# One PSUM tile for the scores of a head pair, with the first bias steps moved between engines and pools

## The chip, the cores and the metric

The kernel runs on one core of a Trainium2 chip. The metric is the device time of one execution in microseconds (us), lower is better. Engines are named as in the profile: PE (TensorE matmul), PEld (its weight loads), DVE (VectorE), ACT (ScalarE), POOL (GpSimd), SP (SyncE, which issues most transfers).

## What is computed

Attention with a learned bias from relative position, then a feed-forward layer. Sizes: 4 batches, 8 heads, 576 positions, head width 64; the feed-forward layer takes 2304 rows of 512 to 2048 and back.

```python
scores = scale * np.matmul(q, k.transpose(0, 1, 3, 2))
x = (np.log1p(np.abs(i - j)) / np.log1p(np.maximum(i, 1)))[..., None]
bias = np.maximum(x @ w1 + b1, 0.0) @ w2          # hidden width 32, 8 heads
scores = scores + bias.transpose(2, 0, 1)[None]
attn = softmax(scores); y = np.matmul(attn, v)    # softmax with its maximum taken off
h = y_rows @ w_in
out = (h / (1 + np.exp(-1.702 * h))) @ w_out
```

## The kernel before, in words

**Precision.** Products of 16-bit operands are made from a high and a low half (q, k, v, weights, softmax rows are each split into two fp16 parts), with three matmuls per product: high by high, high by low, low by high.

**Units.** The attention is cut into 72 units. A unit is one batch, one chunk of 128 query rows (the fifth chunk has 64) and one pair of heads; batches go in two groups of two, 36 units each. Chunks 0 to 3 have eight units in a group, the short chunk four, and a unit of the short chunk takes two pairs of heads. For unit u the loop at line 650 writes, in this order: a hidden step of the bias (`bias_first`), the scores (`emit_s`), the softmax (`emit_soft1`), in units 0 to 3 an extra half step of the bias, one feed-forward step, the product with v for unit u-3 (`emit_av`), another feed-forward step, the second half of the bias step (`bias_second`), the load of the bias rows for unit u+2, weight splits (`weights_to`), and what the dictionary `todo` holds for that unit (loads, transposes and splits of q, k and v).

**Who sets the order.** The written order is a priority. At build time a scheduler (`schedule_with_timeline_sim=True`, line 722) puts the instructions of each engine into a fixed order by its own cost model; on the chip every engine and every DMA queue runs its list in that order and waits where an operand or a buffer isn't ready.

**Scores.** `emit_s` takes two tiles of the PSUM pool `ps_s`, one for each head of the pair. Head 0 has its q and k in partitions 0 to 63, head 1 in partitions 64 to 127, so the matmuls of the two heads use different halves of the PE array's rows. Each head has six matmuls: three parts, each with 512 and with 64 columns (short chunk: twelve). They are written alternately, head 0, head 1, head 0, and so on. DVE then adds the bias rows and takes the extreme (L351), ACT makes the exponential (L358) and the high part (L365, some on DVE at L363), POOL the low part (L366), and a transposing DMA brings the result to `aT` (L371) for `emit_av`.

**PSUM.** `ps_s` has two buffers of two banks, with the tag "s". They are shared by the two score tiles, the transposes of q (`trans_q`) and k (`trans_k`, one head pair at a time) and the products of a bias step (`o`, L176). `ps_h` and `ps_o` have two buffers of one bank; `ps_o` holds the feed-forward output of a block from unit 11 on.

**Bias.** For each of the 36 bias steps (8 for each of four chunks, 4 for the short one) `bias_hidden` makes four hidden tiles, on ACT (L165) or DVE (L167) as the step's string in `BIAS_ENG` says (V or A), `bias_products` multiplies them by w2 on PE (L188 and L190), ACT moves the result out of PSUM (L195) and a DMA of ACT's queue writes it to a table `scr` in DRAM (L196). `bias_load` reads the rows for a unit back (L210, SP's queue). Steps 1 and 2 alone put their products into two one-bank tiles `om` and `ol` (`BIAS_PSUM`). Steps 0 to 7, needed by unit 0, run ahead of the loop, with the entries of `FIRST` written between them; steps 8 to 15 are written in units 0 to 3, two to a unit; the rest from unit 5 on, one to a unit, up to unit 28.

**Weights.** `split_w` loads (L439) and splits (L458, L461, L464, L470, L224) the feed-forward weights in 32 pieces, `W_STEPS` of them in each of units 0 to 11.

Of the kernel before, what the change touches and what calls it, by code (L numbers as in the profile page):

```python
# [7 lines left out]
F32 = mybir.dt.float32  # L8
# [12 lines left out]
def kernel(  # L21
# [26 lines left out]
    nc = tc.nc  # L48
# [21 lines left out]
    BIAS_ENG = ["VVVA" if x % 2 else "VVAA" for x in range(8)] + ["AAAA"] * 16 + ["VVAA"] * 12  # L70
    BIAS_PSUM = {1: "h", 2: "o"}
# [19 lines left out]
    ps_s = ctx.enter_context(tc.tile_pool(name="ps_s", bufs=2, space=PSUM))  # L91
# [80 lines left out]
    def bias_products(c, s, eng, hts, ostag):  # L172
        na = eng.count("A")
        where = BIAS_PSUM.get(8 * c + s)
        if where is None:
            o = ps_s.tile([128, 2, 512], F32, tag="s", name="o").rearrange("p a n -> p (a n)")  # L176
# [23 lines left out]
    def bias_load(u):  # L200
# [6 lines left out]
        for e in range(1 if c < 4 else 2):  # L207
            hh = 2 * (hp + e)
            po = slice(64 * e, 64 * e + scr[c].shape[0])
            nc.sync.dma_start(out=t[po, :], in_=scr[c][:, hh:hh + 2, :].rearrange("p h n -> p (h n)"))  # L210
# [30 lines left out]
    def trans_q(b, c):  # L241
        t = q_st.pop((b, c))
        n = t.shape[0]
        ps = ps_s.tile([128, 2, 512], F32, tag="s", name="qp")[:, 0, 0:NP * n]
# [24 lines left out]
    def trans_k(b, hp):  # L269
        t = k_st[b, hp // 2]  # L270
        ps = ps_s.tile([128, 2, 512], F32, tag="s", name="kp").rearrange("p a n -> p (a n)")
        for c in range(4):
            nc.tensor.transpose(ps[:, 128 * c:128 * c + 128], t[:, hp % 2, c, :], idn)
        nc.tensor.transpose(ps[:, SM:S], kt_st[b][:, hp, :], idn[:ST, :ST])
        d = stage([128, 2, S], F16, "kT", "kT")
        nc.scalar.activation(out=d[:, 0], in_=ps[:, 0:S], func=ACTF.Copy, scale=KS)
        lo_part(False, d[:, 1], ps[:, 0:S], KS, d[:, 0])
        kT[b, hp] = d
# [44 lines left out]
    def emit_s(u):  # L323
# [3 lines left out]
        ps = [  # L327
            ps_s.tile([128, 2, 512], F32, tag="s", name="sp").rearrange("p a n -> p (a n)") for a in range(2)
        ]
# [224 lines left out]
    def drain_to(j):  # L554
# [5 lines left out]
    FIRST = {1: (trans_k, 0, 0), 2: (trans_q, 0, 0), 4: (trans_k, 0, 1), 6: (split_v, 0, 0)}  # L560
    FIRST_UNITS = (
        (0, (trans_q, 1, 0)), (0, (trans_k, 1, 0)), (1, (trans_k, 1, 1)), (1, (load_k, 1, 1)), (2, (split_v, 1, 0)), (2, (trans_k, 0, 2)),
        (2, (load_v, 0, 1)), (3, (trans_k, 0, 3)), (4, (trans_k, 1, 2)), (4, (split_v, 0, 1)), (4, (load_v, 1, 1)),
        (5, (trans_k, 1, 3)), (6, (split_v, 1, 1)),
# [52 lines left out]
    for s in range(8):  # L617
        bias_step(0, s, BIAS_ENG[s], (HT0[(2 * s) % 4], HT0[(2 * s + 1) % 4]), ("os", "bt")[s // 2 % 2])
        if s in FIRST:
            FIRST[s][0](*FIRST[s][1:])  # L620
# [106 lines left out]
```

## Time and profile before

| | |
|---|---|
| median of the runs | 772.23 us (3 runs, 770.73 to 776.1) |
| profiled execution, its own time | 770.94 us |
| its span, first to last instruction | 769.1 us |
| PE busy | 676.4 us, 88% of the span |
| DVE, ACT, POOL busy | 452.3, 425.8, 336.0 us |
| mean granted TensorE clock | 0.923 of full |

The profile is of one execution. Busy time of an engine counts the time in which any of its instructions ran; pipelined matmuls overlap, so the mean duration of one is longer than its share of the busy time. A row of the timeline has the start, the length, the engine, the line, what is written and read, how many instructions were merged, and in brackets the idle time before it and what ended it. Times in a timeline count from the start of the span.

### The profile page before, as it was taken

The numbers are of one execution on the slowest core, as the hardware profiler recorded it, in microseconds if no ns is written. First come the engines' busy times: TensorE is split into PE (matmuls) and PEld (weight loads), VectorE is DVE, ScalarE is ACT, GpSimd is POOL, SyncE is SP. The second block draws the span as 40 slices with busy tenths as digits, with TensorE's granted clock in tenths as the row PEclk, the third lists the DMA queues.
The fourth block names the chain that finished last, engine by engine and source line by source line (L and its number), as shares of the span: only waits on it lengthen the run. The fifth ranks groups of instructions, "written<-read, shape, count | busy, mean of one in ns | idle before, by whom it ended". The sixth has DMA issues, their size and how long they took to land.

```text
span 769.1 us, 17254 instructions
## 1 busy us (share of the span) xinstructions
PE 676.4 (88%) x6648; PEld 413.7 (54%) x6648; DVE 452.3 (59%) x1228; ACT 425.8 (55%) x958; POOL 336.0 (44%) x431
## 2 busy tenths in 40 slices
PE   5347677667999999999999999789999998999997
PEld 2113333224565566566666665456666665667665
DVE  4756678998565565555578964335666564663221
ACT  6667785797566665654456545453544353443123
POOL 1311153423454465455445654436546454563222
PEclk9855675576999999999999999999999999999999
DMA  9766878999956866677588666666685676564000
GB/s 227 225 194 160 242 193 221 287 233 259 229 131 127 177 135 126 153 157 133 106 202 197 129 121 126 138 134 98 143 163 113 111 178 121 98 112 99 15 29 15
DMA packets 249843, 116.50 MB, mean 151 GB/s; under 512 B 229792, under 2 KB 234016, under 8 KB 249760
## 3 DMA queue, kind: packets, MB, share of 16 engines
q1 hardware_dynamic: 241808, 99.96, 62.1%
q10 hardware_dynamic: 7952, 15.43, 6.0%
q8 instruction: 52, 0.85, 0.5%
q14 instruction: 31, 0.25, 0.1%
HBM read 52.85 MB, written 15.34 MB: 89 GB/s over the span
## 4 chain that ended last, share of the span: by engine, by line
PE 58%; DMA 14%; DVE 8%; ACT 4%; issue 3%; POOL 1%; SPq 0%; ACTq 0%; POOLq 0%; DVEq 0%
PE hp L494 20%; PE op L523 20%; DMA aT<-hl 12%; PE sp L335 8%; PE ot L402 6%; DVE a L351 2%; PE ot L395 2%; PE o L188 2%; ACT a L358 1%; ACT hl L365 1%; DVE w L461 1%; DVE th L502 1%; DMA w<-in_moe_w_in_dram 1%; DVE w L464 1%; POOL hl L366 1%
## 5 line engine op out<-in xcount | busy, mean ns | idle before, releaser
L366 POOL TENSOR_TENSOR hl<-a,hl 128x576 f16<-128x576 f32 x142 | 184.4, 1306 | 227.8 <-ACT hl L365 142.9
L494 PE MATMUL hp<-xT,wi 128*128 128x256 f16 (+1 forms) x1920 | 216.1, 263 | 9.1 <-DVE th L502 5.4
L523 PE MATMUL op<-wo,gT 128*128 128x512 f16 x864 | 214.7, 380 | 8.9 <-ACT gT L507 7.1
L494 PEld LDWEIGHTS <-wi 128*128 128x128 f16 x1920 | 167.1, 98 | 50.7 <-issue 20.9
L510 POOL TENSOR_TENSOR gT<-th,gT 128x256 f16<-128x256 f32 (+1 forms) x160 | 101.8, 637 | 131.7 <-DVE gT L509 46.4
L358 ACT ACTIVATE a<-a,mx 128x576 f32<-128x576 f32 x144 | 110.5, 769 | 55.9 <-DVE mx L355 55.0
L351 DVE CUSTOM_DVE_ANT_0 a<-sp,bt 128x576 f32<-128x576 f32 x144 | 106.1, 752 | 41.2 <-PE sp L335 33.4
L502 DVE SCALAR_TENSOR_TENSOR th<-th,hp 128x256 f32<-128x256 f32 (+1 forms) x160 | 62.6, 392 | 114.6 <-ACT th L500 114.2
L335 PE MATMUL sp<-kT,qT 64*128 64x512 f16 (+2 forms) x960 | 114.9, 297 | 15.1 <-DVE kT L224 4.8
L523 PEld LDWEIGHTS <-gT 128*128 128x128 f16 x864 | 80.6, 98 | 80.6 <-ACT gT L507 8.4
L500 ACT ACTIVATE th<-hp 128x256 f32<-128x256 f32 (+1 forms) x160 | 57.0, 357 | 106.9 <-PE hp L494 96.1
L188 PE MATMUL o<-ht,pk 128*32 128x512 f32 x272 | 63.6, 787 | 33.2 <-DVE mx L351 16.9
L335 PEld LDWEIGHTS <-qT 64*128 64x128 f16 (+1 forms) x960 | 45.7, 100 | 78.5 <-issue 50.1
L365 ACT CAST hl<-a 128x576 f16<-128x576 f32 x103 | 67.3, 667 | 35.4 <-DMA aT<-hl 34.7
L165 ACT ACTIVATE ht<-tab,pk 128x576 f32<-128x576 f32 x100 | 81.4, 861 | 3.1 <-PE o L190 2.9
L402 PE MATMUL ot<-v,aT 128*128 128x64 f16 (+1 forms) x1920 | 77.2, 199 | 0.0
L402 PEld LDWEIGHTS <-aT 128*128 128x128 f16 (+1 forms) x1920 | 70.2, 104 | 5.3 <-issue 5.0
L509 DVE CAST gT<-th 128x256 f16<-128x256 f32 x112 | 53.0, 473 | 4.4 <-PE op L523 0.5
L417 POOL TENSOR_TENSOR xn<-xf,xn 128x128 f16<-128x128 f32 x72 | 34.2, 475 | 42.0 <-ACT xn L416 23.4
L416 ACT CAST xn<-xf 128x128 f16<-128x128 f32 x70 | 20.5, 293 | 47.5 <-DVE xf L409 46.3
L386 DVE TENSOR_SCALAR sm<-sm 128x2 f32<-128x2 f32 x72 | 23.9, 332 | 37.8 <-ACT a L358 37.6
L363 DVE CAST hl<-a 128x576 f16<-128x576 f32 x41 | 23.8, 585 | 30.3 <-DMA aT<-hl 21.3
(59 smaller groups left out, 537.4 us busy)
## 6 DMA issues: line engine op xcount, KB each, us to landing
bt<-scr SPq DMA_DIRECT2D x32, 576.0 KB, 4.4
scr<-os ACTq DMA_DIRECT2D x36, 288.0 KB, 3.1
w<-in_moe_w_in_dram SPq DMA_DIRECT2D x16, 512.0 KB, 4.8
w<-in_moe_w_out_dram SPq DMA_DIRECT2D x16, 512.0 KB, 5.2
k<-in_k_dram SPq DMA_DIRECT2D x32, 128.0 KB, 4.3
q<-in_q_dram SPq DMA_DIRECT2D x16, 256.0 KB, 4.4
out_dram<-ob ACTq DMA_DIRECT2D x16, 256.0 KB, 2.5
bt<-scr SPq DMA_DIRECT2D x8, 288.0 KB, 4.2
```

The costliest lines, as they stand in the source:

```text
L165: nc.scalar.activation(out=h, in_=tv, func=ACTF.Relu, bias=b1c, scale=sc[:, col:col + 1])
L188: nc.tensor.matmul(om[po], lhsT=w2b, rhs=h[:, :, 0:128], start=True, stop=True)
L335: nc.tensor.matmul(ps[a][64 * e:64 * e + m, cs], lhsT=qt[r, x, hp + e, 0:m], rhs=kT[b, hp + e][r, y, cs], start=i == 0, stop=i == 2,)
L351: nc.vector.tensor_tensor_reduce(out=at[:, cs], in0=s_ps.pop((u, a))[:, 0:S], in1=bt[:, cs], scale=-1.0 / BS, scalar=3.0e38, op0=ALU.add, ...
L358: nc.scalar.activation(out=at[:, cs], in_=at[:, cs], func=ACTF.Exp, scale=-1.0, bias=mx[:, a:a + 1], accum_out=sm[:, a:a + 1],)
L365: nc.scalar.copy(hl[:, 0, cs], at[:, cs])
L366: (nc.vector if a and u in VEC_EXP_LO else nc.gpsimd).tensor_tensor(out=hl[:, 1, cs], in0=at[:, cs], in1=hl[:, 0, cs], op=ALU.subtract)
L402: nc.tensor.matmul(o[po, 64 * a:64 * a + 64], lhsT=t[:, 9 * y + 5 * a + kb, po], rhs=vt[:, x, 384 * a + 64 * kb:384 * a + 64 * kb + 64], s ...
L494: nc.tensor.matmul(p[:, :n], lhsT=wi16[:, x, cc, 128 * f:128 * f + 128], rhs=r, start=i == 0, stop=i == 11,)
L502: nc.vector.scalar_tensor_tensor(out=g[:, :n], in0=th[:, :n], scalar=1.0, in1=p[:, :n], op0=ALU.add, op1=ALU.mult)
L510: nc.gpsimd.tensor_tensor(out=gt[:, 1, :n], in0=g[:, :n], in1=gt[:, 0, :n], op=ALU.subtract)
L523: nc.tensor.matmul(op_t[j, i], lhsT=gt[:, x, ts], rhs=wo16[:, f, y, :], start=f == 0 and n3 == 0, stop=f == NF - 1 and n3 == 2,)
```

## The change

The two score tiles of a unit become one tile of four banks, and `ps_s` has one such buffer in place of two of two banks. `trans_k` makes both head pairs of a loaded tile into the same kind of tile, so it is called half as often. Bias steps 1 to 19 all use the two one-bank tiles of `ps_o`; step 0 and steps 20 to 35 use the first two banks of a four-bank tile. All eight first steps have three hidden tiles on DVE and one on ACT (before, every second one had two and two). `trans_q(1, 0)`, `trans_k(1, 0)` and `split_v(0, 0)` are written behind the eight first steps and ahead of the loop. The bias rows of unit 0 are loaded by GpSimd's queue. In the loop the weight splits and `bias_first` are written behind `emit_av`.

```diff
--- before.py
+++ after.py
@@ -67,8 +67,8 @@
     BUFS = {"st": 4, "ht": 2, "os": 2, "bt": 2, "a32": 2, "hl": 2, "aT": 2, "xT": 2, "w32": 3, "qT": 3, "kT": 8,
             "v16": 8, "gT": 3, "xn": 2}
 
-    BIAS_ENG = ["VVVA" if x % 2 else "VVAA" for x in range(8)] + ["AAAA"] * 16 + ["VVAA"] * 12
-    BIAS_PSUM = {1: "h", 2: "o"}
+    BIAS_ENG = ["VVVA"] * 8 + ["AAAA"] * 16 + ["VVAA"] * 12
+    BIAS_PSUM = {x: "o" for x in range(1, 20)}
     POOL_V = {(1, 0), (1, 1)}
     VEC_EXP = {u: 1 for u in (*range(33, 42), *range(62, 72))}
     VEC_EXP.update({u: 2 for u in (5, 6, 42, *range(54, 62))})
@@ -88,7 +88,7 @@
     cst = ctx.enter_context(tc.tile_pool(name="cst", bufs=1))
     wk = ctx.enter_context(tc.tile_pool(name="wk", bufs=2))
     dr = ctx.enter_context(tc.tile_pool(name="dr", bufs=1, space=DRAM))
-    ps_s = ctx.enter_context(tc.tile_pool(name="ps_s", bufs=2, space=PSUM))
+    ps_s = ctx.enter_context(tc.tile_pool(name="ps_s", bufs=1, space=PSUM))
     ps_h = ctx.enter_context(tc.tile_pool(name="ps_h", bufs=2, space=PSUM))
     ps_o = ctx.enter_context(tc.tile_pool(name="ps_o", bufs=2, space=PSUM))
 
@@ -173,7 +173,7 @@
         na = eng.count("A")
         where = BIAS_PSUM.get(8 * c + s)
         if where is None:
-            o = ps_s.tile([128, 2, 512], F32, tag="s", name="o").rearrange("p a n -> p (a n)")
+            o = ps_s.tile([128, 4, 512], F32, tag="s", name="o")[:, 0:2].rearrange("p a n -> p (a n)")
             om, ot = o[:, 0:SM], o[:, SM:S]
             outs = [(slice(0, S), o[:, 0:S])]
         else:
@@ -207,7 +207,7 @@
         for e in range(1 if c < 4 else 2):
             hh = 2 * (hp + e)
             po = slice(64 * e, 64 * e + scr[c].shape[0])
-            nc.sync.dma_start(out=t[po, :], in_=scr[c][:, hh:hh + 2, :].rearrange("p h n -> p (h n)"))
+            (nc.sync if u else nc.gpsimd).dma_start(out=t[po, :], in_=scr[c][:, hh:hh + 2, :].rearrange("p h n -> p (h n)"))
         bt_t[u] = t
 
 
@@ -241,7 +241,7 @@
     def trans_q(b, c):
         t = q_st.pop((b, c))
         n = t.shape[0]
-        ps = ps_s.tile([128, 2, 512], F32, tag="s", name="qp")[:, 0, 0:NP * n]
+        ps = ps_s.tile([128, 4, 512], F32, tag="s", name="qp")[:, 0, 0:NP * n]
         for hp in range(NP):
             nc.tensor.transpose(
                 ps[:, n * hp:n * hp + n], t[:, 2 * hp:2 * hp + 2, :].rearrange("p a d -> p (a d)"), idn[:n, :n]
@@ -266,16 +266,18 @@
         nc.sync.dma_start(out=t, in_=k[b, :, SM:S, :].rearrange("h p d -> p h d"))
         kt_st[b] = t.rearrange("p (u a) d -> p u (a d)", a=2)
 
-    def trans_k(b, hp):
-        t = k_st[b, hp // 2]
-        ps = ps_s.tile([128, 2, 512], F32, tag="s", name="kp").rearrange("p a n -> p (a n)")
-        for c in range(4):
-            nc.tensor.transpose(ps[:, 128 * c:128 * c + 128], t[:, hp % 2, c, :], idn)
-        nc.tensor.transpose(ps[:, SM:S], kt_st[b][:, hp, :], idn[:ST, :ST])
-        d = stage([128, 2, S], F16, "kT", "kT")
-        nc.scalar.activation(out=d[:, 0], in_=ps[:, 0:S], func=ACTF.Copy, scale=KS)
-        lo_part(False, d[:, 1], ps[:, 0:S], KS, d[:, 0])
-        kT[b, hp] = d
+    def trans_k(b, e):
+        t = k_st[b, e]
+        pair = ps_s.tile([128, 4, 512], F32, tag="s", name="kp").rearrange("p (u a) n -> p u (a n)", u=2)
+        for u in range(2):
+            ps, hp = pair[:, u, 0:S], 2 * e + u
+            for c in range(4):
+                nc.tensor.transpose(ps[:, 128 * c:128 * c + 128], t[:, u, c, :], idn)
+            nc.tensor.transpose(ps[:, SM:S], kt_st[b][:, hp, :], idn[:ST, :ST])
+            d = stage([128, 2, S], F16, "kT", "kT")
+            nc.scalar.activation(out=d[:, 0], in_=ps, func=ACTF.Copy, scale=KS)
+            lo_part(False, d[:, 1], ps, KS, d[:, 0])
+            kT[b, hp] = d
 
     def load_v(b, e, tag="st"):
 
@@ -324,9 +326,8 @@
         b, c, hp = units[u]
         m, ne = (128, 1) if c < 4 else (64, 2)
         qt = qT[b, c]
-        ps = [
-            ps_s.tile([128, 2, 512], F32, tag="s", name="sp").rearrange("p a n -> p (a n)") for a in range(2)
-        ]
+        pair = ps_s.tile([128, 4, 512], F32, tag="s", name="sp").rearrange("p (h a) n -> p h (a n)", h=2)
+        ps = [pair[:, a] for a in range(2)]
         for i, (x, y) in enumerate(((0, 0), (0, 1), (1, 0))):
             for cs in (slice(0, SM), slice(SM, S)):
                 for e in range(ne):
@@ -557,11 +558,12 @@
 
 
 
-    FIRST = {1: (trans_k, 0, 0), 2: (trans_q, 0, 0), 4: (trans_k, 0, 1), 6: (split_v, 0, 0)}
+    FIRST = {1: (trans_k, 0, 0), 3: (trans_q, 0, 0)}
+    SECOND = ((trans_q, 1, 0), (trans_k, 1, 0), (split_v, 0, 0))
     FIRST_UNITS = (
-        (0, (trans_q, 1, 0)), (0, (trans_k, 1, 0)), (1, (trans_k, 1, 1)), (1, (load_k, 1, 1)), (2, (split_v, 1, 0)), (2, (trans_k, 0, 2)),
-        (2, (load_v, 0, 1)), (3, (trans_k, 0, 3)), (4, (trans_k, 1, 2)), (4, (split_v, 0, 1)), (4, (load_v, 1, 1)),
-        (5, (trans_k, 1, 3)), (6, (split_v, 1, 1)),
+        (0, (load_k, 1, 1)), (1, (split_v, 1, 0)), (2, (trans_k, 0, 1)),
+        (1, (load_v, 0, 1)), (4, (split_v, 0, 1)), (3, (load_v, 1, 1)),
+        (4, (trans_k, 1, 1)), (6, (split_v, 1, 1)),
     )
     BIAS_A = {*range(4), *range(5, 21), 22, 24, 26, 28}
     BIAS_B = set(range(4))
@@ -588,11 +590,11 @@
             n0, n1 = b0 + 2, b0 + 3
             for u, x in (
                 (27, (load_kt, n0)), (28, (load_kt, n1)), (29, (load_k, n0, 0)), (30, (load_k, n1, 0)),
-                (31, (load_v, n0, 0)), (32, (load_q, n0, 0)), (32, (trans_k, n0, 0)), (32, (trans_k, n0, 1)),
-                (32, (load_k, n0, 1)), (33, (load_q, n1, 0)), (33, (trans_k, n1, 0)), (33, (trans_k, n1, 1)),
-                (33, (load_k, n1, 1)), (33, (trans_q, n0, 0)), (34, (trans_k, n0, 2)), (34, (load_v, n1, 0)),
-                (35, (split_v, n0, 0)), (35, (trans_q, n1, 0)), (35, (trans_k, n1, 2)), (35, (trans_k, n0, 3)),
-                (36, (split_v, n1, 0)), (36, (load_v, n0, 1)), (36, (trans_k, n1, 3)), (37, (load_v, n1, 1)),
+                (31, (load_v, n0, 0)), (32, (load_q, n0, 0)), (32, (trans_k, n0, 0)), 
+                (32, (load_k, n0, 1)), (33, (load_q, n1, 0)), (33, (trans_k, n1, 0)), 
+                (33, (load_k, n1, 1)), (33, (trans_q, n0, 0)), (34, (load_v, n1, 0)),
+                (35, (split_v, n0, 0)), (35, (trans_q, n1, 0)), (35, (trans_k, n0, 1)),
+                (36, (split_v, n1, 0)), (36, (load_v, n0, 1)), (36, (trans_k, n1, 1)), (37, (load_v, n1, 1)),
                 (37, (split_v, n0, 1)), (38, (split_v, n1, 1)),
             ):
                 at(o + u, *x)
@@ -618,6 +620,8 @@
         bias_step(0, s, BIAS_ENG[s], (HT0[(2 * s) % 4], HT0[(2 * s + 1) % 4]), ("os", "bt")[s // 2 % 2])
         if s in FIRST:
             FIRST[s][0](*FIRST[s][1:])
+    for x in SECOND:
+        x[0](*x[1:])
     bq = [(c, i) for c in range(1, 5) for i in range(8 if c < 4 else 4)]
     bdone = [8, 0, 0, 0, 0]
 
@@ -648,24 +652,24 @@
     for u in range(BIAS_AHEAD):
         bias_get(u)
     for u in range(NU + AV_LAG):
-        if u in BIAS_A:
-            bias_first()
         if u < NU:
             emit_s(u)
             emit_soft1(u)
-        if u in BIAS_B:
-            bias_second()
-            bias_first()
         ready = NF * sum(1 for x in last_unit if x < u - AV_LAG)
         msteps(ready, STEPS_A.get(u, 1))
         if u >= AV_LAG:
             emit_av(u - AV_LAG)
+        if u < len(W_STEPS):
+            weights_to(w_done[1] + W_STEPS[u])
+        if u in BIAS_A:
+            bias_first()
         msteps(ready, STEPS_B.get(u, 1))
         bias_second()
+        if u in BIAS_B:
+            bias_first()
+            bias_second()
         if u + BIAS_AHEAD < NU:
             bias_get(u + BIAS_AHEAD)
-        if u < len(W_STEPS):
-            weights_to(w_done[1] + W_STEPS[u])
         for fn, args in todo.get(u, ()):
             fn(*args)
     while fpos[1] < len(fq):
```

## Rows read from the trace of the kernel before

**Rows 1.** Busy time by stage: stretch, length, then busy time and count of each engine.

```profile
core 0: us, PE busy (x) PEld busy (x) DVE busy (x) ACT busy (x) POOL busy (x), PEclk, DMA share, GB/s
31.00:44.00 13.00, 0.43 (x4) 0.12 (x2) 7.10 (x13) 2.03 (x4) 0.00 (x0) 0.56 0.77 255
44.00:107.00 63.00, 41.92 (x270) 17.20 (x270) 38.63 (x86) 51.13 (x88) 12.58 (x11) 0.68 0.73 195
107.00:190.00 83.00, 59.76 (x447) 29.19 (x447) 73.28 (x161) 63.07 (x120) 32.56 (x31) 0.61 0.94 243
190.00:700.00 510.00, 491.35 (x5120) 315.07 (x5120) 299.59 (x882) 267.93 (x653) 262.12 (x324) 1.00 0.70 141
```

**Rows 2.** Timeline of PE, two units at 454 to 459 us.

```profile
453.96 0.91 PE L335 MATMUL sp<-kT,qT 64*128 64x512 f16 x6
...
457.83 0.90 PE L335 MATMUL sp<-kT,qT 64*128 64x512 f16 x6
458.66 0.73 PE L402 MATMUL ot<-v,aT 128*128 128x64 f16 x19
```

**Rows 3.** Timeline, scores of one unit and their last read, 430 to 436 us.

```profile
430.69 0.91 PE L335 MATMUL sp<-kT,qT 64*128 64x512 f16 x12
...
435.45 0.75 DVE L351 CUSTOM_DVE_ANT_0 a<-sp,bt 128x576 f32<-128x576 f32 x1
```

**Rows 4.** Timeline of PE, a unit of the short chunk.

```profile
397.44 0.94 PE L335 MATMUL sp<-kT,qT 64*64 64x512 f16 x24
```

**Rows 5.** Busy time by stage of line 335 alone: PE, PEld.

```profile
190.00:700.00 510.00, 83.38 (x799) 33.65 (x798) 1.00 0.70 141
```

**Rows 6.** Timeline, the round of a unit with a bias step, 243 to 254 us.

```profile
243.57 1.06 PE L188 MATMUL o<-ht,pk 128*32 128x512 f32 x8
...
244.79 0.91 PE L335 MATMUL sp<-kT,qT 64*128 64x512 f16 x6
...
244.96 0.74 ACT L195 ACTIVATE os<-o,oc 128x576 f32<-128x576 f32 x1 [1.54 <-PE o L190]
...
253.98 0.39 PE L335 MATMUL sp<-kT,qT 64*128 64x512 f16 x1
```

**Rows 7.** Timeline of the start, from the last of the first bias rows on.

```profile
31.06 0.35 ACTq L196 DMA_DIRECT2D scr<-os  x1
...
36.73 0.80 SPq L210 DMA_DIRECT2D bt<-scr  x2
...
43.37 0.76 DVE L351 CUSTOM_DVE_ANT_0 a<-sp,bt 128x576 f32<-128x576 f32 x1 [2.43 <-DMA bt<-scr]
...
44.19 1.94 PE L188 MATMUL o<-ht,pk 128*32 128x512 f32 x8 [12.76 <-DVE mx L351]
```

**Rows 8.** Groups of instructions, 0 to 45 us: busy time, mean of one (ns).

```profile
L165 ACT ACTIVATE ht<-tab,pk 128x576 f32<-128x576 f32 x16 | 13.2, 872 | 0.1
L167 DVE TENSOR_SCALAR ht<-tab,pk,b1n 128x576 f32<-128x576 f32 x20 | 10.8, 595 | 5.2 <-PE o L190 3.5 <-PE ol L190 1.6
...
L195 ACT ACTIVATE os<-om,oc 128x512 f32<-128x512 f32 x2 | 1.4, 690 | 0.0
...
L195 ACT ACTIVATE os<-ol,oc 128x64 f32<-128x64 f32 x2 | 0.7, 325 | 0.0
```

**Rows 9.** Transfers of the bias rows: issuer, count, size, median us to landing.

```profile
bt<-scr SPq DMA_DIRECT2D x32, 576.0 KB, 4.4
scr<-os ACTq DMA_DIRECT2D x36, 288.0 KB, 3.1
```

**Rows 10.** Groups of ACT's instructions, 44 to 107 us.

```profile
L165 ACT ACTIVATE ht<-tab,pk 128x576 f32<-128x576 f32 x32 | 26.1, 860 | 0.8 <-PE o L190 0.8
...
L195 ACT ACTIVATE os<-o,oc 128x576 f32<-128x576 f32 x8 | 5.8, 720 | 0.0
```

**Rows 11.** Waits: SP's queue from 0 to 60 us, then PE from 44 to 190.

```profile
SPq L210 <- DMA scr<-os: 0.9, 1, 0.9
...
PE o L188 <- DVE mx L351: 16.9, 4, 12.8
```

## The prediction

> **What bounds the kernel now.** I read the busy times by stage first, then the bursts of line 335 on PE, then the start.
>
> The stages [rows 1] show two kernels in one. From 190 us on PE works 491.4 of 510 us at the full granted clock (1.00), while DVE, ACT and POOL are busy a little over half of the time. That stage is bound by PE: a microsecond of PE work taken out there is a microsecond of time, as long as PE doesn't begin to wait. Before 190 us no engine is full throughout. From 31 to 44 us nearly nothing runs on PE (0.4 us) and on ACT (2.0 us of 13). From 44 to 107 us ACT leads with 51.1 of 63 us (81%); from 107 to 190 us DVE leads with 73.3 of 83 us (88%), with the transfers at 0.94. PE has a low granted clock there (0.68, 0.61, that is mostly the lower of its two levels) and isn't the bound.
>
> The bursts of the scores are the central reading. In one unit the two heads run apart: six matmuls in 0.91 us, other work, six more in 0.90 us [rows 2]. In another unit all twelve stand together and take 0.91 us as well [rows 3]; a unit of the short chunk does 24 in 0.94 us [rows 4]. So the second head is free when its matmuls alternate with those of the first, because the two use different halves of the array, and costs a whole burst when they don't. Why they stand apart shows in a round with a bias step [rows 6]: the products `o` hold one of the two buffers, so at 244.79 us only one head's tile is to be had, and the next unit's first head starts again right behind the next products at 253.98.
>
> The start [rows 7]: the last first-step row is sent at 31.06 us, unit 0's bias rows are requested at 36.73, its first subtraction starts at 43.37. PE stands 12.76 us in front of a bias product of the next chunk, because both buffers hold unit 0's scores until DVE has read them. ACT's hidden tiles pile up behind that product.
>
> **The change part by part.**
>
> *Pair tile, stage from 190 us.* Line 335 is busy 83.4 us there for 799 matmuls [rows 5]. At 0.91 us a burst that is 92 bursts. Eight units of the short chunk take 192 of the 799, the other 607 are 50.6 units of twelve: 58.6 units, that is 58.6 bursts if each pair stands together. One tile is had or not had as a whole, and its twelve matmuls are written alternately, so 33 bursts fall away. What one displaces is the time until the next instruction starts, 0.83 us (458.66 less 457.83 [rows 2]). 33 x 0.83 = 27.7 us off the bounding engine. Bounds: at least half, 14, if pairs are still torn apart by other work; at most 33 x 0.91 = 30.
>
> The Trainium skill (TensorE: Matmul & The Clock Gate, Part 3: Packing small matmuls) reports 3.07 times for four row tiles, not four. If a pair here reached the same share of its ideal, it would take 1.30 bursts and give back 58.6 x 0.30 x 0.83 = 15 us of the 28. The trace has the pair itself at 1.00 burst [rows 3], so the row decides and the sum keeps 28.
>
> *One buffer in place of two.* The next user of the tile now waits until both heads have been read. Three users take turns: scores, and for steps 20 to 35 (units 9 to 28) the bias products, and the transposes. A turn of the scores lasts from 430.69 to 436.20, 5.5 us [rows 3], most of it DVE's lag. A turn of the products lasts from 243.57 to 245.70, 2.1 us [rows 6]. Together 7.6 us in a round of 9.2 (244.79 to 253.98 [rows 6]), some 8.4 after the saving, in which PE has feed-forward steps to run. It fits, with less than a microsecond over, and a transpose in the round doesn't fit entirely. I charge 4 us for such waits over the stage, from nothing to 20 x 2 = 40.
>
> *First steps.* Four hidden tiles go from ACT (13.2 / 16 = 0.83 us each) to DVE (10.8 / 20 = 0.54) [rows 8]: ACT -3.3, DVE +2.2 us; DVE has its waits for PE there to hide it. Taking a result out of PSUM in two pieces costs 0.69 + 0.325 in place of about 0.72 [rows 8, 10]: +0.29 us of ACT for 17 more steps, 1.5 of it here. With one pair of `ps_o` banks a step follows the one before by 1.06 us of products [rows 6] and 0.69 of ACT, some 2 us with the hand-overs; ACT's own work for a step is 0.83 + 1.02 = 1.85. Eight steps from about 6.5 us thus end between 24 and 30; I take 26, 5 us earlier than 31.06. What was written between them and now stands behind (`split_v`, two transposes) runs in the wait for the bias rows, where ACT is idle [rows 1].
>
> *Bias rows of unit 0 by GpSimd's queue.* SP's request waited only 0.9 us longer for the table rows than for its own queue [rows 11], so at most that is to be had; POOL is idle from 31 to 44 us [rows 1], so a POOL that waits there holds up nothing. I take 0. From last row sent to first subtraction it was 12.3 us [rows 7]; the medians of the two transfers make 7.5 [rows 9]. I take 11.3, with the weight loads as competitors. Unit 0 starts its softmax at 37, 6 us earlier (0 to 12).
>
> The Trainium skill (DMA: Bandwidth & Descriptors, Latency and other measured facts) gives a transfer of GpSimd's queue a first byte at about 1 us in place of 0.6. By it this edit would cost 0.4 us, and the sum would be as much later; no row here has such a transfer.
>
> *Bias steps 8 to 19 outside of the score pool.* PE no longer stands in front of their products; the waits on the subtraction are 16.9 us in all before 190 us, 12.8 of them the one at 44 [rows 11]. In the wait for unit 0's rows ACT can make hidden tiles of the next chunk: I put 5 us of the 26.1 + 5.8 us of bias work of the next stage [rows 10] there, and 1.9 us of the transposes that moved ahead, against 8 x 0.29 = 2.3 us more. ACT's 51.1 us become 46.5, and at the same 81% the 63 us become 57.4: 5.6 us. Bounds: none of it, with the 2.3 us on top, to 10 us.
>
> *Units 4 to 12.* Bound by DVE and the transfers [rows 1], which the change doesn't relieve. The scores' bursts at the low clock stand in the chain of a unit at times: 2 us (0 to 6). The new places of `bias_first` and the weight splits in the written order change priorities alone; I take 0, between -3 and +3.
>
> Sum: 28 + 6 + 5.6 + 2 - 4 = 37.6 us. From the profiled execution's 770.9 us that gives 733, and the execution stands 1.3 us under the runs' median of 772.2, so I say 734.
>
> **The rivals.**
>
> *The stage becomes bound by something else* (aT's transposing DMA, the gT chain through DVE, ACT and POOL). For it: PE already waits some 18 us in 510 [rows 1]. Against: no other engine is over 60%, the transfers are at 0.70. If half of the 28 us comes back as waits: 748.
>
> *The ramp loses instead of gains*: step follows step through one pair of banks, and the one score tile is also the transposes'. If the first 190 us get 10 us longer instead of 14 shorter, 758.
>
> *The halves stay apart in the list*, the change doesn't do what it says: then 28 + 2 are missing, 764. Against it: both halves come with one tile.
>
> *Slower: the single buffer becomes the bound of units 9 to 28.* If DVE reads the second head not 5.5 but 10 us after the burst, the turns make 12 us in each of 20 rounds in place of 8.4, about 72 us against the gain, 805. It decides from 20 waits of 1.9 us on, a lag of some 8 us. Against it: the lag of 5.5 was taken where DVE had no reason to hurry, and the scheduler can put feed-forward work between.
>
> The Trainium skill (Trainium Kernel Development and Optimization, Best Practices) advises double-buffering and reads constant bubbles as a sign that PSUM ran out. By it the pool of one buffer goes this rival's way; no run here shows it yet.
>
> **How the numbers follow.** Forecast 0.71, around 734 (720 to 746); other bound 0.11; ramp loses 0.06; halves apart 0.05; slower 0.07. 1% (7.7 us) is about what a measurement of this kernel can tell from no change. Faster by more than that are the first three, 0.88; within it the halves apart, 0.05; slower 0.07. The range of 8 in 10 goes from 718 (all terms good: 30 + 12 + 10, less some) to 756, which takes in the other bound and most of the ramp's case.
>
> **What would show it.** Right: line 335 in the PE-bound stage at some 53 us, nearly all bursts of twelve at 0.91 us, and that stage about 24 us shorter; unit 0's first subtraction at about 37 us, no wait of PE over 10 us near it, the stage of PE at full use from about 176 us. Wrong: bursts of six remain; waits of line 335 or 188 on DVE or ACT of more than a few us in that stage; the first subtraction at 43 us or later; PE's clock below 1.00 in the stage, which the trace of before never shows there, even in stretches where PE waits.

## The result and the profile after

| | before | after |
|---|---|---|
| median of the runs, us | 774.16 (4 runs) | 751.3 (4 runs, 749.64 to 756.88) |
| ratio after / before | | 0.9722, 95% interval 0.9654 to 0.979 |
| profiled execution, its own time, us | 770.94 | 752.68 |
| its span, us | 769.1 | 750.7 |
| first feed-forward matmul on PE, us | 180.8 | 163.1 |
| from there to PE's last matmul, us | 583.8 | 582.8 |
| PE idle in that stretch, us | 18.7 | 37.4 |

The change is worth 2.8%, some 22 us, where 37.6 were predicted. A time beside a ratio, here and below, is the median of the runs; the ratio is worked out from the runs themselves, and leaves out two executions of the kernel before with both PSUM edits that fell into a slower state (789 us). Everything that is read by stage comes from one execution of each kernel, and executions of one kernel lie up to 7 us apart (749.64 to 756.88), so a difference of a few us between two stages is not certain by itself. The last three lines of the table, here and below, are worked out from the matmuls in order of their start: each counts until the next one starts, and what is left until the next start is idle. They say at once where the prediction went wrong: the stage that was to become about 24 us shorter (28 by the pair tile, less 4) became 1.0 us shorter, and the start, which was to give some 14 us, gave 17.7.

The busy times by stage of the kernel after (columns as in [rows 1]):

```profile
core 0: us, PE busy (x) PEld busy (x) DVE busy (x) ACT busy (x) POOL busy (x), PEclk, DMA share, GB/s
31.00:44.00 13.00, 7.49 (x59) 3.09 (x60) 8.01 (x13) 11.61 (x20) 0.75 (x1) 0.87 1.01 322
44.00:100.00 56.00, 34.97 (x258) 15.00 (x256) 40.31 (x90) 50.23 (x101) 19.07 (x21) 0.80 0.86 233
100.00:177.00 77.00, 39.33 (x368) 22.30 (x368) 66.97 (x142) 49.58 (x94) 30.25 (x21) 0.63 0.96 223
177.00:680.00 503.00, 469.33 (x5142) 305.77 (x5141) 302.24 (x892) 270.46 (x660) 265.83 (x324) 0.99 0.71 145
```

Against [rows 1]: the hole from 31 to 44 us is filled (ACT 11.6 us where it had 2.0), ACT is now 90% busy in the stage behind it, and PE, which had work for 491 of 510 us in its own stage, has it for 469 of 503.

The scores' line is 336 now. Its busy time in the stretch of [rows 5] (PE, PEld), and one of its bursts on PE's timeline with what follows it, to be held against [rows 2]:

```profile
190.00:700.00 510.00, 55.35 (x792) 22.67 (x792) 0.99 0.69 139
```

```profile
457.15 0.91 PE L336 MATMUL sp<-kT,qT 64*128 64x512 f16 x12 [0.34 <-DVE qT L224]
458.00 0.84 PE L495 MATMUL hp<-xT,wi 128*128 128x128 f16 x12
```

Twelve matmuls take 0.91 us, and the line's busy time falls from 83.38 to 55.35 us. Of its 792 matmuls there 708 stand in whole pairs (43 bursts of twelve and 8 of 24); the others are torn by other work. What PE waits for in its stage is the other half (waits of PE in the kernel after, 190 to 700 us: total, times, longest):

```profile
PE hp L495 <- DMA xT<-xn: 6.9, 7, 2.0
PE hp L495 <- DVE th L503: 6.0, 4, 2.7
PE ot L396 <- DMA aT<-hl: 4.5, 5, 1.3
PE ot L396 <- DVE th L503: 4.1, 3, 2.3
PE op L524 <- ACT ob L534: 2.1, 2, 1.7
PE qp L246 <- DVE mx L352: 1.5, 1, 1.5
```

The same view of the kernel before:

```profile
PE op L523 <- ACT gT L507: 7.1, 4, 2.6
PE hp L494 <- DVE th L502: 5.4, 6, 1.3
PE ot L395 <- DVE th L502: 3.0, 3, 2.0
PE op L523 <- POOL gT L510: 1.8, 3, 0.8
PE sp L335 <- DVE qT L224: 1.1, 1, 1.1
```

Before, PE never waited there for a transposing DMA; after, it waits 11.4 us for `xT` and `aT`.

### The profile page after: what moved, and what is told of

The parts are those of the page before. It is cut to its first block, busy times and chain, and to the rows that moved or that the text cites. A ratio compares the mean times of both kernels' runs of the same rounds, so it can differ in the third digit from the quotient of the medians.

```text
span 750.7 us, 17318 instructions
## 1 busy us (share of the span) xinstructions
PE 634.1 (84%) x6648; PEld 400.8 (53%) x6648; DVE 454.5 (61%) x1232; ACT 422.5 (56%) x971; POOL 342.9 (46%) x432
## 4 chain that ended last, share of the span: by engine, by line
PE 45%; DMA 24%; DVE 13%; ACT 8%; issue 5%; POOL 3%; SPq 1%; ACTq 0%; DVEq 0%; POOLq 0%
PE hp L495 17%; DMA aT<-hl 15%; PE op L524 15%; PE ot L403 5%; DVE a L352 4%; PE sp L336 3%; ACT a L359 3%; DMA xT<-xn 3%; POOL hl L367 2%; DMA w<-in_moe_w_in_dram 2%; PE ot L396 2%; ACT ht L165 1%; ACT hl L366 1%; PE o L188 1%; DVE w L462 1%
## 5 line engine op out<-in xcount | busy, mean ns | idle before, releaser
L367 POOL TENSOR_TENSOR hl<-a,hl 128x576 f16<-128x576 f32 x142 | 190.3, 1351 | 157.4 <-ACT hl L366 81.4
L352 DVE CUSTOM_DVE_ANT_0 a<-sp,bt 128x576 f32<-128x576 f32 x144 | 103.1, 753 | 33.3 <-PE sp L336 25.3
L336 PE MATMUL sp<-kT,qT 64*128 64x512 f16 (+2 forms) x960 | 71.8, 295 | 16.0 <-DVE mx L352 5.2
L165 ACT ACTIVATE ht<-tab,pk 128x576 f32<-128x576 f32 x96 | 78.1, 863 | 5.0 <-PE ol L190 5.0
L366 ACT CAST hl<-a 128x576 f16<-128x576 f32 x103 | 65.7, 666 | 23.8 <-DMA aT<-hl 23.6
L403 PEld LDWEIGHTS <-aT 128*128 128x128 f16 (+1 forms) x1920 | 71.3, 105 | 3.7 <-issue 3.0
L336 PEld LDWEIGHTS <-qT 64*128 64x128 f16 (+1 forms) x960 | 29.1, 99 | 59.8 <-issue 28.8
L387 DVE TENSOR_SCALAR sm<-sm 128x2 f32<-128x2 f32 x72 | 30.9, 430 | 44.0 <-ACT a L359 43.8
L396 PE MATMUL ot<-v,aT 128*128 128x128 f16 (+1 forms) x240 | 28.6, 230 | 33.0 <-DMA aT<-hl 27.9
L188 PE MATMUL om<-ht,pk 128*32 128x512 f32 x152 | 40.1, 719 | 10.1 <-ACT os L195 10.1
L510 DVE CAST gT<-th 128x256 f16<-128x256 f32 x112 | 46.1, 417 | 3.8
L396 PEld LDWEIGHTS <-aT 128*128 128x128 f16 (+1 forms) x240 | 17.4, 103 | 49.0 <-DMA aT<-hl 34.6
```

The costliest lines, as they stand in the source:

```text
L165: nc.scalar.activation(out=h, in_=tv, func=ACTF.Relu, bias=b1c, scale=sc[:, col:col + 1])
L336: nc.tensor.matmul(ps[a][64 * e:64 * e + m, cs], lhsT=qt[r, x, hp + e, 0:m], rhs=kT[b, hp + e][r, y, cs], start=i == 0, stop=i == 2,)
L352: nc.vector.tensor_tensor_reduce(out=at[:, cs], in0=s_ps.pop((u, a))[:, 0:S], in1=bt[:, cs], scale=-1.0 / BS, scalar=3.0e38, op0=ALU.add, ...
L366: nc.scalar.copy(hl[:, 0, cs], at[:, cs])
L367: (nc.vector if a and u in VEC_EXP_LO else nc.gpsimd).tensor_tensor(out=hl[:, 1, cs], in0=at[:, cs], in1=hl[:, 0, cs], op=ALU.subtract)
L396: nc.tensor.matmul(o[po, 0:128], lhsT=t[:, 9 * y + 4, po], rhs=vt[:, x, 256:384], start=i == 0, stop=False, skip_group_check=True,)
```

## The experiments

Each ratio is to runs of the kernel before on the same chip, taken with it. The question that they had to settle: 28 us of PE work had gone, as predicted, and the time had not. Either something else bounds that stage, or the single score buffer takes back what the pairing gives; and where does the earlier start come from?

| kernel | us | ratio, 95% interval |
|---|---|---|
| changed, heads written one after the other | 757.39 | 0.9793, 0.9746 to 0.984 |
| changed, unit 0's rows by SP | 755.05 | 0.976, 0.9722 to 0.9797 |
| before + pair tile | 801.94 | 1.0359, 1.0313 to 1.0405 |
| changed, old order in the loop | 750.65 | 0.9696, 0.9645 to 0.9746 |
| changed, late bias products in `ps_h` | 764.07 | 0.9869, 0.9793 to 0.9946 |
| changed, half transposes | 733.33 | 0.9445, 0.9383 to 0.9506 |
| changed, one product of three | 727.29 | 0.9378, 0.9328 to 0.9428 |
| before + bias steps 1 to 19 in `ps_o` | 756.32 | 0.9765, 0.971 to 0.982 |
| before + both PSUM edits | 779.99 | 1.0086, 1.0046 to 1.0126 |
| changed, weights spread over 17 units | 755.55 | 0.9732, 0.968 to 0.9784 |
| the same, old order in the loop | 751.47 | 0.9704, 0.9666 to 0.9742 |
| changed, two score tiles again | 753.64 | 0.9716, 0.9674 to 0.9758 |

**Heads one after the other.** The tile stays, the order of the twelve matmuls goes.

```diff
-        for i, (x, y) in enumerate(((0, 0), (0, 1), (1, 0))):
+        for a, (i, (x, y)) in ((a, z) for a in range(2) for z in enumerate(((0, 0), (0, 1), (1, 0)))):
+            r = slice(64 * a, 64 * a + 64)
...
-                    for a in range(2):
-                        r = slice(64 * a, 64 * a + 64)
```

> The changed kernel with one thing undone: inside the pair tile the twelve matmuls are written head by head, six of head 0 and then six of head 1, so that the two halves of the array do not work together. Theory A (the concurrency takes 25 us off PE after 190 us, but about half of it comes back as waits for late operands, so PE is no longer the only bound): about 12 us slower than the changed kernel (763), line 335/336 busy some 83 us in the PE-bound stage again, PE idle there lower by some 12 us. Theory B (PE bounds the stage fully, the missing gain lies in the start alone): 25 to 30 us slower (778), PE idle unchanged.

A burst on PE's timeline of this kernel:

```profile
429.94 1.17 PE L335 MATMUL sp<-kT,qT 64*128 64x512 f16 x12
```

The dose was smaller than meant: 1.17 us, not two times 0.91. Score work behind the first feed-forward matmul rises from 54.0 to 71.8 us, the idle time falls from 37.4 to 29.2, and that stretch gets 6.3 us longer. So a third of the PE work put in shows in the time of that stage, as far as two single executions tell: the ratios of the two kernels, 0.9793 and 0.9722, have intervals that overlap.

**One product of three.** Two thirds of the score matmuls go, with tile, turns and buffers as they are.

```diff
-        for i, (x, y) in enumerate(((0, 0), (0, 1), (1, 0))):
+        for i, (x, y) in enumerate(((0, 0),)):
...
```

> The changed kernel with one of the three products of the scores (high by high), two thirds of the score matmuls left out: about 0.55 us less of PE in each unit, some 32 us in the stage from 177 us. Theory A (PE is no longer the only bound there, about a third to a half of PE's work comes through): 10 to 16 us faster than the changed kernel (735 to 741), PE idle higher by the rest. Theory B (PE bounds the stage): 30 us faster (721). Theory C (something else sets the pace wholly): 0 to 4 us.

Score work there falls by another 30.7 us (54.0 to 23.3), and the stretch from 582.8 to 563.4: 19.4 us, some two thirds. PE work taken out of this stage does pay, more than the third to a half that was expected for a stage that PE bounds only in part. That speaks against a stage that something else bounds altogether, and the 28 us of the pairing should have shown in part at least.

**The two PSUM edits, apart and together, on the kernel before.** First the pair tile alone:

```diff
-    ps_s = ctx.enter_context(tc.tile_pool(name="ps_s", bufs=2, space=PSUM))
+    ps_s = ctx.enter_context(tc.tile_pool(name="ps_s", bufs=1, space=PSUM))
...
+        pair = ps_s.tile([128, 4, 512], F32, tag="s", name="sp").rearrange("p (h a) n -> p h (a n)", h=2)
+        ps = [pair[:, a] for a in range(2)]
```

> The kernel before with the pair tile alone: one score buffer of four banks, used also by all bias products that used the score pool, transposes one head pair at a time, nothing moved. Theory A: the stage bound by PE gives its 12 us net, and the start loses a few us since the bias products of steps 3 to 19 now wait for the only buffer: 765 to 770. Theory B (the pair is all of the gain, the other edits give nothing): 751. Theory C (the single buffer needs the other edits, its waits eat the gain): 774 or more.

It costs 3.6%, some 27 us. Its stage from 44 to 107 us, to be held against [rows 1], and its waits of PE from 0 to 180 us:

```profile
44.00:107.00 63.00, 24.78 (x186) 11.02 (x187) 32.82 (x73) 34.73 (x63) 8.42 (x7) 0.55 0.61 173
```

```profile
PE o L188 <- ACT os L195: 19.6, 7, 4.1
PE o L188 <- DVE mx L350: 15.0, 5, 4.5
PE o L188 <- DVE mx L354: 13.6, 2, 11.1
PE sp L334 <- DVE kT L224: 10.2, 5, 3.0
```

Products, scores and transposes stand in one queue for one buffer: ACT, at 51.1 us in [rows 1], has 34.7. Then the bias products of steps 1 to 19 in `ps_o` alone (`BIAS_PSUM = {x: "o" for x in range(1, 20)}` in the kernel before):

> The kernel before with one part of the change alone: bias steps 1 to 19 put their products into the two one-bank tiles, the scores keep two tiles in two buffers. Theory A (the pair tile pays through PE, this part only clears the way for it): 765 to 770, the waits of line 188 on the subtraction before 130 us gone, pairs together up to unit 8 and apart behind. Theory B (this part is the gain, and the pair tile adds little to it): 752 to 756.

One line gives most of the whole change: 2.35%, some 18 us. PE's first feed-forward matmul starts at 155.4 us, 25 earlier, with 8.3 us of bias products more behind it (25.1 in place of 16.8). From 44 to 107 us:

```profile
44.00:107.00 63.00, 50.53 (x314) 21.65 (x315) 47.76 (x108) 53.73 (x104) 21.05 (x20) 0.70 0.86 226
```

PE, DVE and POOL each do 8 to 9 us more in that stretch than in [rows 1]: the units go ahead, which the products had held up (unit 3's first subtraction starts at 71.7 us where it was 92.7). Both edits together:

> The kernel before with the two PSUM parts of the change together, pair tile and bias steps 1 to 19 in the one-bank tiles, and nothing else (transposes of k one head pair at a time, first steps, queue and loop as before). Alone they gave 802 and 756. Theory A (these two are the change; the pair tile's single buffer costs nothing once the bias products are out of it, and PE's saving shows in part): 748 to 752, as the changed kernel. Theory B (the moved first steps, paired transposes and the new order are needed beside them): 757 to 765.

1.0086 is slower than either expectation: on top of the `ps_o` line the pair tile still costs 3.2% (1.0086 less 0.9765), some 25 us.

**Two score tiles again in the changed kernel.** Each of the two transposes of a pair of k then takes a tile of its own as well; everything else stays.

```diff
-    ps_s = ctx.enter_context(tc.tile_pool(name="ps_s", bufs=1, space=PSUM))
+    ps_s = ctx.enter_context(tc.tile_pool(name="ps_s", bufs=2, space=PSUM))
...
-        pair = ps_s.tile([128, 4, 512], F32, tag="s", name="sp").rearrange("p (h a) n -> p h (a n)", h=2)
-        ps = [pair[:, a] for a in range(2)]
+        ps = [
+            ps_s.tile([128, 2, 512], F32, tag="s", name="sp").rearrange("p a n -> p (a n)") for a in range(2)
+        ]
```

> The changed kernel with only the pair tile undone: each head's scores stand in a tile of their own again (two buffers of two banks each), and the k transposes of a pair use such a tile each; everything else of the change stays. Theory A (the single score buffer costs at the start about what the pairing saves later, so the pairing is worth next to nothing in the whole change): 748 to 753 us, as the changed kernel, with score work near 80 us again after the first feed-forward matmul and that matmul some 15 us earlier than the changed kernel's 163. Theory B (the pairing is still a net gain): 757 to 762 us, the first feed-forward matmul no earlier than 158 us. Theory C (the pairing is a net cost in the full set): 745 us or less, the first feed-forward matmul near 145 us.

0.9716 against 0.9722: the pair tile, for which the change is named, is worth nothing that these intervals show (some 6 us either way) within the full set. The time is within 1 us of what was expected for that; the first feed-forward matmul comes 9.2 us earlier, not 15. From the first feed-forward matmul on, us:

| | scores | bias products | rest of PE | idle | stretch | first matmul at |
|---|---|---|---|---|---|---|
| two tiles | 81.3 | 26.1 | 469.8 | 15.6 | 592.9 | 153.9 |
| pair tile | 54.0 | 18.0 | 473.4 | 37.4 | 582.8 | 163.1 |

The pairing takes 27.3 us of scores off PE, and 21.8 come back as idle time. The rest of PE takes 3.6 us more, and the 8.1 us of bias products only lie on the other side of the first matmul, which comes 9.2 us later. PE's waits from 177 to 690 us with two tiles:

```profile
PE hp L495 <- DVE th L503: 7.1, 9, 1.4
PE op L524 <- ACT gT L508: 4.5, 3, 2.4
...
PE hp L495 <- DMA xT<-xn: 0.4, 1, 0.4
```

With the pair tile `xT` and `aT` make 11.4 us there, here 0.4. A reading that goes with it is the lead, the time between a unit's first subtraction and its product with v (the starts of lines 352 and 396, mean over units 18 to 27): 28.8 us with two tiles, 28.7 before, 15.9 with the pair tile. The softmax runs some 13 us less ahead of the feed-forward work. That its transposing DMAs come late more often for this reason is argued, not shown. Of the 21.8 us some 15 lie ahead of unit 36's product with v (418 us), where the lead is shorter, and some 7 behind it, where the lead is about as long as with two tiles (28 to 34 us against 29 to 33, units 36 to 63). And in the run with the late bias products in `ps_h` (below) the lead is 44.5 us, and PE is idle for 47.0 us all the same.

**What holds the one tile.** The start of units 2 to 6 of the changed kernel shows it. PE's timeline:

```profile
61.25 1.09 PE L275 MATMUL kp<-idn,k 128*128 128x128 f32 x4 [4.99 <-issue]
...
67.36 0.64 PE L275 MATMUL kp<-idn,k 128*128 128x128 f32 x4
...
74.40 0.50 PE L396 MATMUL ot<-v,aT 128*128 128x128 f16 x3 [4.17 <-DMA aT<-hl]
...
80.92 0.91 PE L336 MATMUL sp<-kT,qT 64*128 64x512 f16 x12 [1.31 <-DVE kT L224]
```

and DVE's:

```profile
65.22 0.74 DVE L224 SCALAR_TENSOR_TENSOR kT<-kp,kT 128x576 f16<-128x576 f32 x1
...
79.65 0.29 DVE L410 TENSOR_TENSOR xf<-ot,rv 128x128 f32<-128x128 f32 x1 [4.06 <-PE ot L403]
79.98 0.23 DVE L415 CAST xn<-xf 128x128 f16<-128x128 f32 x1
80.12 0.75 DVE L224 SCALAR_TENSOR_TENSOR kT<-kp,kT 128x576 f16<-128x576 f32 x1
```

The transposes of one pair of k take the tile at 61.25. The second low part, which sets it free, stands in DVE's list behind `xf`, `xf` waits for the product with v, and that for `aT`'s transposing DMA. The instruction that makes the high part stands in ACT's list in the same way: it starts at 71.84, and PE had done the transposes at 68.19. The tile comes free at 80.87, and unit 3's scores start at 80.92. So a turn of the transposes lasts 19.6 us, and unit 3's first subtraction comes 24.9 us behind unit 2's (59.7 and 84.6). The next turns of this kind are 91.17 to 103.29 (k), 106.89 to 117.70 (q) and 129.27 to 132.63 (q), and each time the next scores start within 0.15 us: 45.9 of the 71.4 us up to 132.63 no scores can start. With two tiles the pair of k still fills both, for 10.0 us from 55.52 on and for 12.9 from 75.14 on, but q takes only one of them: one head's scores start right behind its transposes, and the other head's when q's tile comes free at 99.77 (PE's timeline of that kernel):

```profile
90.46 1.11 PE L246 MATMUL qp<-idn,q 128*128 128x128 f32 x4
91.66 1.62 PE L336 MATMUL sp<-kT,qT 64*128 64x512 f16 x6
...
99.82 0.91 PE L336 MATMUL sp<-kT,qT 64*128 64x512 f16 x6 [1.58 <-DVE qT L224]
```

Unit 6's first subtraction is at 103.1 us there and at 119.8 with the pair tile. These lines are from the start. What shortens the lead in units 18 to 27 they do not show; that it grows when bias steps 20 to 35 leave the score tile points at the turns of those products.

**Half transposes.** If `aT` is in that circle, a shorter transpose must show at the start. The product with v reads the high half twice, so the low half is missing from the result, and PE's work stays.

```diff
-        nc.sync.dma_start_transpose(out=t, in_=hl.rearrange("p x n -> p (x n)"))
+        nc.sync.dma_start_transpose(out=t[:, 0:9], in_=hl[:, 0])
...
```

> The changed kernel with only the high half of the softmax rows transposed (half of the bytes of each of the 72 transfers to aT); the product with v then uses the high half in place of the low one, so the low part is left out of the result and PE does as many matmuls as before. Theory A (after the pair tile the pace hangs on the chain through the transfers, whose share is 0.9 up to 177 us and whose landings end the longest waits): 20 us faster or more (730), first feed-forward matmul before 155 us, waits on aT and xT gone. Theory B (DVE and ACT hold the start, PE the rest): within 5 us of the changed kernel.

The transposes from 44 to 177 us (count, median us to landing), this kernel, then the changed one:

```profile
aT<-hl SPq DMA_TRANSPOSE x12, 5.1
```

```profile
aT<-hl SPq DMA_TRANSPOSE x11, 7.4
```

The first feed-forward matmul comes at 148.4 us, 14.7 earlier, at the same PE work, and the stretch behind it is 4.4 us shorter (578.4). So most of the gain lies at the start, which waits for these transposes. The transfers as a whole get lighter, too, but the others land about as before (weight loads in 4.8 us where it was 5.0 and 5.3, q rows in 4.9 where it was 4.1), so it is the transposes' own length that tells. DVE and ACT run as many instructions in both kernels; neither alone was the limit of that stage. One thing expected did not come: behind the start PE waits for `xT` and `aT` as before (12.4 us from 177 to 690, 11.4 in the changed kernel).

**Other suspects.** The weight splits are DVE's largest work at the start; `W_STEPS = [1] + [2] * 15 + [1]` spreads them over 17 units, with the new order and with the old one:

> The changed kernel with the 32 weight pieces spread over units 0 to 16, two to a unit, instead of three to a unit up to unit 11. Theory A (units 4 to 12 are bound by DVE and the transfers, 0.87 and 0.96 busy from 100 to 177 us, much of it weight pieces; later units have DVE at 0.6): 8 to 15 us faster than the changed kernel (736 to 743), first feed-forward matmul near 152 us. Theory B (the chain from unit to unit through aT sets that stage): within 3 us. Theory C (feed-forward matmuls then wait for weights): slower.

> The same spreading on the changed kernel with the loop's written order as before. Theory A: as the run beside it, within 4 us. Theory B (the order matters once the weights no longer fill the stage): more than 5 us apart from it.

Neither gains (0.9732 and 0.9704 against 0.9722 and 0.9696, the ratio of the old order without the spreading). The old order in the loop by itself:

> The changed kernel with the written order of the loop as before (bias hidden step ahead of the scores, weight splits at the end). Theory A (the order is a priority only, and the scheduler pulls ready work forward either way): within 3 us of the changed kernel (748 to 754). Theory B (the new order is what shortened the start, ACT doing the softmax ahead of hidden tiles): 6 to 10 us slower, first feed-forward matmul near 172 us instead of 163.

No difference that its interval shows. The first feed-forward matmul does come earlier with the old order in both pairs (156.9 against 163.1 us, and 156.3 against 161.9 with the weights spread), so the new order is no part of the earlier start. Unit 0's rows by SP again:

> The changed kernel with the bias rows of unit 0 loaded by SP's queue again. Theory A (GpSimd's queue made this transfer late: issued at 38.4 us, landed 7.7 us later, against 4.6 us for the one by SP beside it): first subtraction at 43 us instead of 46.8, and what of that reaches the end depends on the stage up to 177 us; if that stage hangs on the chain from unit 0, 3 us faster (748). Theory B (that stage is bound by the transfers, whose share is 0.93 over it): first subtraction 3 us earlier, total unchanged within 1 us.

The first subtraction comes at 42.62 us, 4.1 earlier, and the time does not follow: 0.976. The late bias products out of the score tile, into `ps_h`:

> The changed kernel with bias steps 20 to 35 taken out of the score tile too: their products go to the two one-bank buffers of the feed-forward hidden tile and the product with v. Theory A (turns on the one score tile cost PE some 5 us of waits between 163 and 350 us, and the rest of the lost gain lies with late transposes and the feed-forward chain): 3 to 6 us faster than the changed kernel (746), waits of line 188 on the subtraction gone, some new waits of hidden tiles. Theory B (the single score tile is what holds units 9 to 28): 15 us faster or more (736). Theory C (the two buffers it moves to are fuller than the one it leaves): slower, 755 or more.

It loses 12 us. Other waits take the place of those that go (PE, 177 to 690 us): the hidden tiles of the feed-forward layer, which share `ps_h` with the products now, wait for ACT's copy of them, and the scores wait more for the score tile.

```profile
PE hp L495 <- DVE th L503: 7.9, 9, 3.7
PE sp L336 <- DVE mx L352: 5.0, 7, 1.5
...
PE hp L495 <- ACT os L195: 3.4, 5, 0.9
```

## Why the prediction held only in part

**Pair tile, 28 us: the work right, the time wrong.** Whole pairs, twelve in 0.91 us, line 336 at 55.35 us where some 53 were forecast, and 27.3 us less on PE: each step of that count held. The pair packs without loss, as the row had said. By the prediction's estimate from the 3.07 of four that the Trainium skill (TensorE: Matmul & The Clock Gate, Part 3: Packing small matmuls) reports, half of it would have been left; the measured burst decides. The step that failed is the one ahead of it, that a microsecond of PE work out of this stage is a microsecond of time "as long as PE doesn't begin to wait". It began to: 21.8 of the 27.3 us came back. A part of that is a general price of this stage: with the single tile kept, heads apart gave back 8.2 us of idle time for 17.8 us of PE work put in, and one product cost 8.8 for 30.7 taken out. An estimate by these two rates puts 8 to 13 us of the 21.8 to that price and leaves 9 to 14 to the single buffer, on which the two kernels compared differ.

**Single buffer, 4 us: the term that was mis-sized, and looked for in the wrong place.** The sum looked at units 9 to 28 and at PE's waits for the tile itself; those are small (`o`, `qp` and `sp` behind `mx`, some 5 us from 177 to 690 us). One part of the price lies at the start (the first feed-forward matmul 9.2 us later than with two tiles), the other in PE's idle time behind it. The pair tile alone costs 27 us net on the kernel before. The prediction named the turn of the transposes in half a sentence ("a transpose in the round doesn't fit entirely") and took its length from nowhere; three of four turns at the start last 11 to 20 us, because the instructions that end a turn stand behind others in the lists of ACT and DVE. The rival of the ramp had the right place and the right user ("the one score tile is also the transposes'"), at 0.06, though the start as a whole gained; the rival of the single buffer had the right cause with the wrong stage. The Trainium skill (Trainium Kernel Development and Optimization, Best Practices) says that consistent bubbles can mean that PSUM ran out; the pair tile alone, at 1.0359 with PE's waits for the one buffer, agrees.

**Bias products out of the score pool, 5.6 us with the hole: too small.** The `ps_o` line alone gives 18 us. The 12.76 us wait of [rows 7] was read as a loss in ACT's hidden tiles alone; it also held up the units behind it, and the stage's 81% of ACT, which the sum kept, became 90%.

**First steps, 6 us: wrong, and worth nothing.** The last row was to go out at 26 us; it went at 32.74, and the first subtraction started at 46.76, 3.4 later than before. The issues and the subtraction in the kernel after:

```profile
32.74 0.36 ACTq L196 DMA_DIRECT2D scr<-os  x1
...
37.86 0.34 SPq L210 DMA_DIRECT2D bt<-scr  x1
...
38.38 0.75 POOL L210 DMA_DIRECT2D bt<-scr  x1 [10.35 <-DVE w L465]
...
46.76 0.75 DVE L352 CUSTOM_DVE_ANT_0 a<-sp,bt 128x576 f32<-128x576 f32 x1
```

What was written behind the first steps did not run behind them: ACT makes v's splits and the next chunk's first hidden tiles between the last three results (from 23.6 us on). The written order is only a priority. As a gain the term would have been empty, though: 4.1 us earlier (rows by SP) did not shorten the run.

**GpSimd's queue, 0.** Its transfer landed 7.7 us after the issue, where SP's next to it took 4.6. With two tiles it was 6.8 on GpSimd's queue and 7.1, the median of two, on SP's, so the traces do not show that the queue is the cause. The Trainium skill (DMA: Bandwidth & Descriptors, Latency and other measured facts) has a first byte at about 1 us in place of 0.6 for GpSimd's queue; a difference of 0.4 us is not to be told from these landings. The time shows no gain by either.

**Units 4 to 12 and the order of the loop, 2 and 0.** The order made no difference. The transposes set the pace of that stage more than DVE did, which the prediction had taken from the busy shares.

**The sum** came out at 37.6 where 22 were measured. That 751.3 lies in the range of 8 in 10 (718 to 756) is luck in part; it lies outside the narrower band given with the forecast (720 to 746). Two errors went against each other: the bias products gave about 12 us more than put down, the pairing with its buffer 24 less; the first steps gave nothing of their 6. The rival with the nearest time, a stage bound by something else (748), named `aT`'s transposing DMA and half the gain lost; the waits for `xT` and `aT` are there, but the loss is more than half.

**What the rest of the change is worth** follows from the same ratios. On top of both PSUM edits the other parts give 3.6% (1.0086 to 0.9722, some 28 us); without the pair tile 0.5% (0.9765 to 0.9716), which the intervals do not separate from nothing. They seem to repair mostly what the single buffer breaks. Neither the loop's order nor the queue is the one that does it; among the paired k transposes, the work moved ahead of the loop and the hidden tiles on DVE it stays open. Also open is how much of the 21.8 us is the smaller lead, if it is that at all, and how much PE's waits for the tile itself. A pair tile with the transposes in another pool was not tried.

## What to carry to other kernels

Before two PSUM buffers are merged into one, list everyone who takes a turn in that pool, and measure each turn up to the instruction that frees it, along the list of the engine that runs it; the slow turn may be that of a rare user. Work taken off the bounding engine can come back as its idle time (here 21.8 of 27.3 us), so read its idle time, and how far ahead the producers run, before and after. A one-line edit that takes a producer out of a shared pool can be worth more than the change it was made for; run the parts alone.

## What the runs showed of the hardware

- PE overlapped the two row halves even with all matmuls of one half listed ahead of the other's: twelve in 1.17 us, between 0.91 (alternating) and two times 0.91. The first matmul of the second head, seventh in the list, started some 0.26 us after the first one and ahead of the fourth in the list (0.47 us at the earliest).
- A transposing DMA of half the size landed in 5.1 us in place of 7.4 (medians) while the transfers were busy at the start; it was shorter by a third, not by half.
- Issuing the transfer of the bias rows kept POOL for 0.75 us, SP's queue for 0.52 (median of 39, from 0.32 to 1.23).
- The granted clock of the changed kernel, in a stage where that of before never left 1.00, fell to half, the lower of its two levels, for 3.4 us at 481 and at 566 us. Just before, PE had stood still for 2.3 and 2.7 us. The prediction had put this down as a sign of being wrong; at half speed the two stretches cost some 3.4 us together, by estimate.
